# A token and channel mixer behind threshold attention: four small rearrangements in place of an interleaved second token layer

## The chip, the cores and the metric

The kernel runs on one core of a Trainium2 chip. A core has five engines that run beside each other and meet at semaphores: TensorE (PE, matmuls and transposes into PSUM), VectorE (DVE), ScalarE (ACT), GpSimd (POOL) and SyncE (SP, which here only issues DMAs). The metric is the device time of one launch in microseconds (us).

## The reference

Eight batch rows, eight heads, 576 tokens, 64 channels a head. Attention keeps only scores within `tau` of their row's maximum, and its output, put together to `[8, 576, 512]`, goes through a mixer with a token MLP (576 to 256 to 576) and a channel MLP (512 to 1536 to 512), each with a residual:

```python
scores = scale * q @ k.T
thresh = max(scores, -1) - tau
scores = where(scores >= thresh, scores, -1e9)
attn = softmax(scores);  x = attn @ v            # heads side by side: (8, 576, 512)
h = relu(x.T @ w_tok1) @ w_tok2                  # over tokens
u = x + h.T
out = u + relu(u @ w_ch1) @ w_ch2                # over channels
```

q, k, v are float32. The four weights are float64 and reach the kernel as 64-bit words, so they are converted to float32 on the chip.

## The kernel before

Work runs through *units*: 128 rows of scores for two heads, 18 units to a batch row, 144 in all (`u`; `t = u % 9`). In unit `u` the loop makes the scores of `u`, normalizes `u - 1`, and turns the weights of `u - 2` (`w`), so that they can be multiplied by the values when three units are together. Batch row 0 turns on PE (`turn`), the others on DVE in 32x32 blocks with DMAs behind them (`turn_blocks`). From row 1 on the mixer's steps of the row before are handed out between these by `fill`, each with a cost against a quota.

Loading queries and keys, and what runs at the start:

```python
nc.scalar.dma_start(out=tau_sb, in_=...)             # first on ACT's queue
def load_qk(n, eng, parts=range(8)):                 # part: 32 channels of one head, of q or k
    ...
        eng[which].dma_start(out=loaded[n][which][32*i : 32*i+32], in_=(q, k)[which][b, 2*p+h, :, 32*c : 32*c+32]...)
load_qk(0, (nc.sync, nc.scalar))                     # q on SP, k on ACT
... # five small DVE operations on tau_sb -> toff, ntau
def prep(n):                                         # q, then k, whole: 128x576 each
    for src, name in ((lq, "qT"), (lk, "kT")):
        nc.vector.transpose(out=sb, in_=src...)
prep(0)
```

Converting the weights: 31 pieces, each in three parts; `weight(n)` does the next n parts. Part 0 and 1 of piece i+1 stand on ACT beside the parts of piece i on DVE:

```python
def on_scalar(i, part):
    if part == 0: nc.scalar.activation(out=lo, in_=lo, func=AF.Copy, scale=2.0**-29)        # L193
    else:         nc.scalar.activation(out=h2, in_=hi, func=AF.Abs)                         # L195
def on_vector(i, part):
    if part == 0:   nc.vector.tensor_scalar(out=h2, in0=h2, ... max, mult)                  # L203
    elif part == 1: nc.vector.tensor_scalar(out=bits, in0=h2, ... shift)                    # L205
    else:           nc.vector.scalar_tensor_tensor(out=bits, in0=hi, ..., in1=bits)         # L209
def on_gpsimd(i):   nc.gpsimd.tensor_tensor(out=dst, in0=dst, in1=lo, op=ALU.add)           # L217
```

`h2` is one buffer (`high`) for all pieces. One pass of the loop, cut:

```python
scores(u)                    # PE matmuls L304; DVE maxima L309; POOL bias L310
...; norm(u - 1)             # DVE rr L333, L334; POOL L337
if b_now: weight(2)
...
if back and not in_blocks(wb):
    for i in range(3): turn(w, i)      # PE tr L355, copy to eT on DVE or ACT, L357
if b_now: fill(0.4)
if back and in_blocks(wb): turn_blocks(w)    # DVE L367, 16 DMAs L376
if b_now: weight(2)
weigh(u)                     # ACT Prelu L319, Exp L326, with fill(0.2) between
if b_now: weight(2)
```

The mixer: `turn_x` (PE tx L447, ACT copy L448) and `tok1` (PE L454), then `tok2`, whose add into xT is on DVE; `channel_mlp` has `ch1` (PE L510, ACT Relu L511) and `ch2` (PE L532, DVE add L544 or copy L550, store L551). PSUM for these comes from pools of two buffers.

```python
def tok2(c, f):              # 288 tokens (half f) of 128 channels (c): two matmul pairs, L464
    ...; nc.vector.tensor_add(out=u, in0=u, in1=to)                                         # L468
steps += [(0.97, lambda: tok2(c, f)) for f in range(2) for c in ps]
...
last = steps[-half:]; del steps[-half:]      # push(b): the second halves (f = 1) ...
for i, step in enumerate(steps):             # left-over steps of the row before go between
    n = (3 if b == 1 or (b % 2 == 0 and i == waits[1]) else 2) if i in waits else 1
    todo.extend(old[:n] + [step]); del old[:n]
...
for i, step in enumerate(last): new.insert(2*i + 1, step)    # ... stand between ch1 steps
```

`ch2` runs in parts of J = 3 products, but J = 1 in the second group of row pair 0.

Of the kernel before, what the change touches and what calls it, by code (L numbers as in the profile page):

```python
# [21 lines left out]
def kernel(  # L22
# [63 lines left out]
    UB = 9 * NP // 2  # L86

    tau_sb = const.tile([P, 1], F32, name="tau_sb")
    nc.scalar.dma_start(out=tau_sb, in_=bass.AP(tensor=tau.tensor, offset=0, ap=[[0, P], [1, 1]]))


    loaded = {}
    VL = 4
    vlast = [const.tile([P, P], F32, name=f"vl{i}") for i in range(VL)]

    def load_qk(n, eng, parts=range(8)):


        b, p = pairs[n]
        if n not in loaded:  # L100
            loaded[n] = [ld.tile([P, S // 32, 32], F32, tag=tag, bufs=1, name=f"{tag}_{n}") for tag in ("lq", "lk")]
        for part in parts:
            i, which = divmod(part, 2)
            h, c = divmod(i, 2)
            eng[which].dma_start(
                out=loaded[n][which][32 * i : 32 * i + 32],
                in_=(q, k)[which][b, 2 * p + h, :, 32 * c : 32 * c + 32].rearrange("(n t) d -> t n d", t=32),
            )

    def load_v(n):  # L110
# [8 lines left out]
    make_identity(nc, ident)  # L119
    for t in vlast:  # L120
        nc.gpsimd.memset(t, 0.0)
    load_qk(0, (nc.sync, nc.scalar))

    w1 = const.tile([P, NT, DTOK], F32, name="w1")
    w2 = const.tile([P, NTK, S], F32, name="w2")
# [10 lines left out]
    WMAX = 512  # L136
    scratch = work.tile([P, NP * 2 * S], U32, tag="xT", name="scratch")
    NRAW = 4
    high = scratch[:, 2 * WMAX * NRAW : 2 * WMAX * NRAW + WMAX].bitcast(F32)
    raw_at = [scratch[:, 2 * WMAX * i : 2 * WMAX * (i + 1)] for i in range(NRAW)]  # L140

    def like(x, dst):
# [26 lines left out]
    def load_piece(i):  # L169
        if i >= len(pieces):  # L170
            return
        dst, src = pieces[i]
        rows = dst.shape[0]
        n = 1
        for d in dst.shape[1:]:
            n *= d
        raw = raw_at[i % NRAW][0:rows, 0 : n * (2 if wide(i) else 1)].bitcast(src.dtype)
        nc.sync.dma_start(out=like(raw, dst), in_=src)
        if wide(i):
            words = raw.bitcast(U32).rearrange("p (n w) -> p n w", w=2)  # L180
            h2 = high[0:rows, 0:n]
            raws[i] = like(words[:, :, 0], dst), like(words[:, :, 1], dst), like(h2, dst)
        else:
            raws[i] = like(raw, dst)
# [77 lines left out]
    tlow = const.tile([P, 1], F32, name="tlow")  # L262
    toff = const.tile([P, 1], F32, name="toff")
    ntau = const.tile([P, 1], F32, name="ntau")
    nc.vector.tensor_scalar(out=tlow, in0=tau_sb, scalar1=0.0, scalar2=-3.0e38, op0=ALU.is_lt, op1=ALU.mult)
    nc.vector.tensor_scalar(out=toff, in0=tau_sb, scalar1=0.0, scalar2=FAR, op0=ALU.max, op1=ALU.min)
    nc.vector.tensor_scalar(out=toff, in0=toff, scalar1=-1.0 / SCALE, scalar2=None, op0=ALU.mult)
    nc.vector.tensor_add(out=toff, in0=toff, in1=tlow)
    nc.vector.tensor_scalar(out=ntau, in0=toff, scalar1=SCALE, scalar2=None, op0=ALU.mult)


    heads = {}
# [5 lines left out]
    def in_blocks(b):  # L278
        return b > 0

    def prep(n):
        lq, lk = loaded.pop(n)
        made = []
        for src, name in ((lq, "qT"), (lk, "kT")):
            sb = work.tile([P, S], F32, tag=name, name=f"{name}_{n}")
            nc.vector.transpose(out=sb, in_=src.rearrange("p n d -> p (n d)"))  # L286
            made.append(sb)
        heads[n] = made

    def scores(u):  # L290
        b, p0, t = units[u]
# [136 lines left out]
    def token_mlp(b, ps=range(NP)):  # L428

        xT = xTs[b]  # L430
        o = S * (b % 2)
        L = len(ps)
        cols = slice(P * ps[0], P * ps[0] + P * L)
        if b not in hidden:
            hidden[b] = work.tile([P, NTK, DM], F32, tag="a", bufs=1, name=f"a_{b}")
        a = hidden[b]

        def psum(name):
            return (ps_mm or ps_tr).tile([P, DM], F32, tag="mm" if ps_mm else "tr", name=name)

        def turn_x(t, n):
            M = MT[t]
            to = ps_tr.tile([P, MAIN], F32, tag="tr", name=f"tx_{b}_{t}_{ps[0]}")[0:M, 0 : n * L * P].rearrange("p (t c x) -> p t c x", t=n, c=L)
            for i in range(n):
                for c in range(L):
                    tok = o + (t + i) * P
                    nc.tensor.transpose(out=to[:, i, c, :], in_=xT[:, ps[c], tok : tok + M], identity=ident)  # L447
            nc.scalar.copy(out=x_sb[0:M, t : t + n, cols], in_=to.rearrange("q t p d -> q t (p d)"))  # L448

        def tok1(m):  # L450
            need(2)
            to = psum(f"t1_{b}_{m}_{ps[0]}")[:, 0 : P * L]
            for t in range(NT):
                nc.tensor.matmul(to, lhsT=w1[:, t, P * m : P * m + P], rhs=x_sb[:, t, cols], start=(t == 0), stop=(t == NT - 1))  # L454
            if ps_mm:
                nc.scalar.activation(out=a[:, m, cols], in_=to, func=AF.Relu)
            else:
                copies.append(lambda: nc.vector.tensor_scalar(out=a[:, m, cols], in0=to, scalar1=0.0, scalar2=None, op0=ALU.max))

        def tok2(c, f):  # L460
            need(6)
            to = psum(f"t2_{b}_{c}_{f}")[:, 0:HS]
            for m in range(NTK):
                nc.tensor.matmul(  # L464
                    to, lhsT=a[:, m, P * c : P * c + P], rhs=w2[:, m, HS * f : HS * f + HS], start=(m == 0), stop=(m == NTK - 1)
                )
            u = xT[:, c, o + HS * f : o + HS * f + HS]
            nc.vector.tensor_add(out=u, in0=u, in1=to)  # L468

        n = NI // L  # L470
        steps = [(0.11 * n * L, lambda t=t: turn_x(t, n)) for t in range(0, NI, n)] + [(0.11 * L, lambda: turn_x(NI, 1))]
        first = len(steps)
        steps += [(1.1 * L, lambda m=m: tok1(m)) for m in range(NTK)]
        steps += [(0.97, lambda c=c, f=f: tok2(c, f)) for f in range(2) for c in ps]
        return steps, (first, first + NTK)


# [4 lines left out]
    def channel_mlp(b, uT, i):  # L482
# [1 line left out]
        s = {}  # L484
        n = min(GR, 2 * S - GR * i)
        nt = n // P


        J = 1 if b == 0 and i == 1 else 3

        def turn_u():

# [22 lines left out]
                    s["ut"] = work.tile([P, GR // P, 4, NCC * 32], F32, tag="ut", bufs=1, name=f"ut_{b}_{i}")  # L515
                    turn_u()

        def ch2(t, part, J):

            need(7 + NJ + J * part + J - 1)  # L520
            t0 = GR * i + P * t
            if part == 0:
                s["ps"] = ps_mm.tile([P, NCC, P], F32, tag="mm", name=f"c2_{b}_{i}_{t}")
# [7 lines left out]
            for j in range(J * part, J * part + J):  # L531
                nc.tensor.matmul(  # L532
                    flat,
                    lhsT=s["g"][:, j, P * t : P * t + P],
                    rhs=wc2[:, j, :],
                    start=(j == 0 and b > 0),
                    stop=(j == NJ - 1),
                    skip_group_check=True,
                )
            if J * part + J == NJ:  # L540
                o = s["us"][:, t].rearrange("q a x -> q (a x)")
                if b:
                    move_u()
                    nc.vector.tensor_add(  # L544
                        out=o.rearrange("q (c k d) -> q c k d", c=NCC, k=4),
                        in0=ps.rearrange("q c (k d) -> q c k d", k=4),
                        in1=s["ut"][:, t].rearrange("q k (c d) -> q c k d", c=NCC),
                    )
                else:
                    nc.vector.tensor_copy(out=o, in_=flat)  # L550
                nc.sync.dma_start(out=out[b : b + 2].rearrange("b s d -> (b s) d")[t0 : t0 + P, :], in_=o)  # L551

        return [(0.0067 * n, lambda j=j: ch1(j)) for j in range(NJ)] + [
            (0.867 * J + (0.0 if part or b else 0.4), lambda t=t, part=part: ch2(t, part, J)) for t in range(nt) for part in range(NJ // J)
        ]

    def move_u():
# [25 lines left out]
    def push(b):  # L583
        nonlocal quota
        uT = xTs[b]
        steps, waits = token_mlp(b) if b else token_mlp(b, range(NP // 2, NP))
        half = NP if b else NP // 2
        last = steps[-half:]
        del steps[-half:]
        old = list(todo)  # L590
        todo.clear()
        todo.extend(early)
        early.clear()

        for i, step in enumerate(steps):
            n = (3 if b == 1 or (b % 2 == 0 and i == waits[1]) else 2) if i in waits else 1
            todo.extend(old[:n] + [step])
            del old[:n]
        todo.extend(old)
        new = []  # L600
        for i in range(2) if b % 2 == 0 else range(2, (2 * S + GR - 1) // GR):
            new.extend(channel_mlp(b - b % 2, uT, i))

        for i, step in enumerate(last):
            new.insert(2 * i + 1, step)
        todo.extend(new)
        quota = (sum(c for c, _ in todo) - (KEEP if b else KEEP_FIRST)) / (UB - 1)

    prep(0)
    due = deque()  # L610
    b_now = 0
    LAG = 2
# [13 lines left out]
    for u in range(len(units) + LAG + 4):  # L626
# [18 lines left out]
            early.popleft()[1]()  # L645
        if 0 < u <= len(units):
            norm(u - 1)
        if b_now:
            weight(2)
        else:  # L650


# [21 lines left out]
        if back and in_blocks(wb):  # L674
            turn_blocks(w)
        if b_now:
            weight(2)
        if on and (b_now or not visit):
            weigh(u)
        elif b_now:  # L680
# [60 lines left out]
```

## Time and profile before

| | before |
|---|---|
| time, median of 3 | 1360.13 us (1359.4 to 1361.83) |
| span of the profiled execution | 1360.0 us |
| PE busy | 1310.5 us (96%) |
| DVE, ACT, POOL busy | 590.9, 584.4, 354.8 us |
| half-clock stretches of PE[...] | near 100, 114, 141 and 250 us |

PE's busy time against the span says how much room is left, and the stretches show where it is. A row of the waits names who waited for whom, the total, the number of times and the longest. In the timeline a row has its start, its length, the engine with the line of the kernel, what it writes and reads, and in brackets the idle time of that engine ahead of it with what ended it. SPq and ACTq are DMA issues.

### The profile page before, as it was taken

What the parts mean: (1) busy time and instruction counts of PE and PEld (TensorE: products, weight loads), DVE (VectorE), ACT (ScalarE), POOL (GpSimd) and SP (SyncE); (2) the same over time, 40 slices, a digit from 0 to 9 for tenths busy, and PEclk for the clock granted to TensorE, in tenths of its full rate; (3) what the DMA queues carried; (4) which work ended last, traced back from release to release, by engine and by line L of the source; (5) the groups of instructions that cost most, each with busy time, mean ns of one, the idle gap of its engine ahead of it and who ended that gap; (6) DMA issues with size and microseconds to landing.
All of it is one profiled execution on the core that took longest, in us unless ns stands there. A gap on an engine that the chain in (4) does not pass through costs nothing.

```text
span 1360.0 us, 17797 instructions
## 1 busy us (share of the span) xinstructions
PE 1310.5 (96%) x6138; PEld 812.2 (60%) x6138; DVE 590.9 (43%) x1024; ACT 584.4 (43%) x1299; POOL 354.8 (26%) x683
## 2 busy tenths in 40 slices
PE   6888899999999999999999999999999999999998
PEld 4555656547474666565665567465757566576675
DVE  5878874445343553435244445434443454201000
ACT  5776654454454444443434534353434454220110
POOL 4665652222222221222122222222221222100000
PEclk9998999999999999999999999999999999999999
DMA  5434764545454444444344435534443452400000
GB/s 122 109 90 125 203 157 103 127 95 124 93 126 99 104 112 100 112 110 100 82 104 110 116 83 124 124 81 113 110 101 83 113 117 76 112 24 22 18 24 32
DMA packets 296538, 135.31 MB, mean 99 GB/s; under 512 B 204736, under 2 KB 289216, under 8 KB 296448
## 3 DMA queue, kind: packets, MB, share of 16 engines
q1 hardware_dynamic: 167840, 118.15, 34.1%
q10 hardware_dynamic: 128608, 16.01, 7.4%
q8 instruction: 49, 0.80, 0.3%
q14 instruction: 41, 0.34, 0.1%
HBM read 43.25 MB, written 9.44 MB: 39 GB/s over the span
## 4 chain that ended last, share of the span: by engine, by line
PE 82%; DVE 5%; DMA 4%; ACT 3%; SPq 3%; issue 1%; POOL 1%; ACTq 0%; DVEq 0%; POOLq 0%
PE c L532 26%; PE c L510 24%; PE sc L304 10%; PE pv L416 8%; PE t L454 5%; PE t L464 4%; PE pv L411 3%; DVE mx L309 2%; SPq L376 2%; DMA lq<-in_q_dram 2%; ACT e L319 1%; SPq L500 1%; PE tx L447 1%; DMA lk<-in_k_dram 1%; ACT e L326 1%
## 5 line engine op out<-in xcount | busy, mean ns | idle before, releaser
L309 DVE TENSOR_REDUCE mx<-sc 128x1 f32<-128x576 f32 x288 | 204.4, 750 | 488.6 <-PE sc L304 488.5
L510 PE MATMUL c<-xT,wc 128*128 128x256 f32 (+1 forms) x1920 | 402.3, 362 | 6.2 <-DVE xT L468 3.3
L532 PE MATMUL c<-wc,g 128*128 128x512 f32 x864 | 388.8, 597 | 0.0
L510 PEld LDWEIGHTS c<-xT,wc 128*128 128x128 f32 x1920 | 333.7, 190 | 73.9 <-issue 24.2
L310 POOL TENSOR_SCALAR bias<-mx,toff 128x1 f32<-128x1 f32 x288 | 83.2, 289 | 781.8 <-DVE mx L309 725.5
L532 PEld LDWEIGHTS c<-wc,g 128*128 128x128 f32 x864 | 158.6, 190 | 184.2 <-issue 182.2
L319 ACT ACTIVATE e<-sc,bias 128x576 f32<-128x576 f32 x288 | 199.3, 740 | 151.4 <-POOL bias L310 147.1
L511 ACT ACTIVATE g<-c 128x256 f32<-128x256 f32 (+1 forms) x240 | 87.0, 363 | 314.7 <-PE c L510 307.8
L326 ACT ACTIVATE e<-e,ntau 128x576 f32<-128x576 f32 x288 | 221.3, 772 | 0.0
L337 POOL TENSOR_SCALAR e<-e,rr 128x576 f32<-128x576 f32 x288 | 215.1, 760 | 14.1 <-DVE rr L334 3.3
L304 PE MATMUL sc<-kT,qT 64*128 64x288 f32 (+1 forms) x1280 | 194.2, 440 | 12.2 <-DVE kT L286 7.3
L367 DVE STREAM_TRANSPOSE T<-e 128x1152 f32<-128x1152 f32 x126 | 171.9, 1364 | 5.2 <-DMA eT<-T 2.1
L304 PEld LDWEIGHTS sc<-kT,qT 64*128 64x128 f32 (+1 forms) x1280 | 107.1, 180 | 98.0 <-issue 54.6
L416 PE MATMUL pv<-eT,lv 128*64 128x384 f32 (+1 forms) x1024 | 138.6, 411 | 0.0
L416 PEld LDWEIGHTS pv<-eT,lv 128*64 128x64 f32 x1024 | 77.8, 139 | 49.5 <-issue 42.9
L421 ACT COPY xT<-pv 128x384 f32<-128x384 f32 (+1 forms) x56 | 21.0, 401 | 180.2 <-PE pv L416 172.9
L544 DVE TENSOR_TENSOR us<-c,ut 128x512 f32<-128x512 f32 x27 | 18.7, 692 | 156.0 <-PE c L532 135.4
L464 PE MATMUL t<-w,a 128*128 128x288 f32 x256 | 76.3, 422 | 1.4 <-DVE xT L468 1.3
L454 PE MATMUL t<-x_sb,w 128*128 128x512 f32 (+1 forms) x180 | 73.8, 558 | 0.0
L464 PEld LDWEIGHTS t<-w,a 128*128 128x128 f32 x256 | 46.4, 192 | 22.2 <-issue 10.6
L326 ACT ACTIVATION_READ_ACCUMULATOR e<-e,ntau 128x1 f32 x288 | 56.9, 198 | 0.0
L411 PE MATMUL pv<-eT,vl 128*64 128x384 f32 (+1 forms) x256 | 46.6, 433 | 10.5 <-DMA lq<-in_q_dram 3.6
(46 smaller groups left out, 525.6 us busy)
## 6 DMA issues: line engine op xcount, KB each, us to landing
eT<-T SPq DMA_DIRECT2D x672, 108.0 KB, 2.3
scratch<-in_moe_w_ch_dram SPq DMA_DIRECT2D x24, 512.0 KB, 3.7
lv<-in_v_dram SPq DMA_DIRECT2D x32, 288.0 KB, 3.3
out_dram<-us SPq DMA_DIRECT2D x36, 256.0 KB, 2.2
lk<-in_k_dram ACTq DMA_DIRECT2D x111, 72.0 KB, 2.8
lq<-in_q_dram ACTq DMA_DIRECT2D x106, 72.0 KB, 2.3
ut<-us SPq DMA_DIRECT2D x192, 32.0 KB, 1.9
lq<-in_q_dram SPq DMA_DIRECT2D x22, 72.0 KB, 3.3
```

The lines of the kernel that those rows point to most:

```text
L304: nc.tensor.matmul(sc[h][rows, f, 0:HS], lhsT=qT[r, cols], rhs=kT[r, HS * f : HS * f + HS], start=True, stop=True)
L309: nc.vector.tensor_reduce(out=mx[:, c], in_=sc[h][:, :, 0:HS], axis=AX.XY, op=ALU.max)
L319: nc.scalar.activation(out=eh, in_=sc[h][:, :, 0:HS], func=AF.Prelu, bias=bias[:, h : h + 1], scale=SCALE, alpha=STEEP)
L326: nc.scalar.activation(out=eh, in_=eh, func=AF.Exp, bias=ntau, accum_out=rs[:, h : h + 1])
L337: nc.gpsimd.tensor_scalar(out=eh, in0=eh, scalar1=rr[:, h : h + 1], scalar2=1.0, op0=ALU.mult, op1=ALU.mult)
L367: nc.vector.transpose(out=T[:, :, place, :].rearrange("p a (c x) -> p c a x", c=NK), in_=e.rearrange("p (c a x) -> p c a x", c=NK, a=4))
L411: nc.tensor.matmul(to[r], lhsT=vl[:, r], rhs=e[NI], start=True, stop=False, skip_group_check=True)
L416: nc.tensor.matmul(to[r], lhsT=lv[:, j, :], rhs=e[j], start=False, stop=(c == NI - 1), skip_group_check=True)
L454: nc.tensor.matmul(to, lhsT=w1[:, t, P * m : P * m + P], rhs=x_sb[:, t, cols], start=(t == 0), stop=(t == NT - 1))
L464: nc.tensor.matmul(to, lhsT=a[:, m, P * c : P * c + P], rhs=w2[:, m, HS * f : HS * f + HS], start=(m == 0), stop=(m == NTK - 1))
L510: nc.tensor.matmul(ps, lhsT=wc1[:, j, c, :], rhs=uT[:, c, GR * i : GR * i + n], start=(c == 0), stop=(c == NCC - 1))
L532: nc.tensor.matmul(flat, lhsT=s["g"][:, j, P * t : P * t + P], rhs=wc2[:, j, :], start=(j == 0 and b > 0), stop=(j == NJ - 1), skip_group_ ...
```

## The change

There are five parts. The last takes something out again that the kernel before had.

- **First unit's queries.** The first 128 queries are loaded by DMAs of their own and transposed alone ahead of the keys; the other 448 follow, on the same queue. `tau` is loaded behind the keys, and its five DVE operations come behind the transposes.
- **Two places for absolute values.** `high` becomes a buffer of twice the size; piece i uses half `i % 2`. It lies in space that the channel MLP takes later.
- **Row 0's last turns.** In units 18 and 19, in which row 0's last two units are turned, the first `weight(2)` moves behind the turns, as `weight(4)` with the one that stood there.
- **Last tile in column halves.** The second channel layer of the last 128 tokens runs as twelve products of 256 columns, add and store, and then the same for the other 256.
- **The token MLP's second layer** is not split any more: its steps run channel group by channel group, both halves in turn, all ahead of the channel MLP. The special cases of n and J go.

```diff
-    load_qk(0, (nc.sync, nc.scalar))
+    load_qk(0, (nc.sync, nc.scalar), blocks=(range(P // 32), range(S // 32)))
+    load_qk(0, (nc.sync, None), range(0, 8, 2), blocks=(range(P // 32, S // 32), None))
+    nc.scalar.dma_start(out=tau_sb, ...)
...
-    high = scratch[:, 2 * WMAX * NRAW : 2 * WMAX * NRAW + WMAX].bitcast(F32)
+    high = work.tile([P, GR // P, 4, NCC * 32], F32, tag="ut", bufs=1, name="high")...
...
-            h2 = high[0:rows, 0:n]
+            h2 = high[0:rows, WMAX * (i % 2) : WMAX * (i % 2) + n]
...
+        for which, lo, hi in ((0, 0, first), (1, 0, S // 32), (0, first, S // 32)):   # prep(0, 4)
+            if lo < hi: nc.vector.transpose(out=heads[n][which][:, 32*lo : 32*hi], in_=srcs[which][:, lo:hi]...)
...
-        steps += [(0.97, lambda c=c, f=f: tok2(c, f)) for f in range(2) for c in ps]
+        steps += [(0.97, lambda c=c, f=f: tok2(c, f)) for c in ps for f in range(2)]
...
-        J = 1 if b == 0 and i == 1 else 3
...
+        def ch2_last(half):
+            ps = ps_mm.tile([P, w], F32, tag="mm", ...)                    # w = 256
+            for j in range(NJ): nc.tensor.matmul(ps, lhsT=s["g"][:, j, 0:P], rhs=wc2[:, j, w*half : w*half + w], ...)
+            if half == 0: move_u()
+            nc.vector.tensor_add(out=o..., in0=ps..., in1=s["ut"]...)
+            nc.sync.dma_start(out=out[...][t0 : t0 + P, w*half : w*half + w], in_=o)
...
-            n = (3 if b == 1 or (b % 2 == 0 and i == waits[1]) else 2) if i in waits else 1
+            n = 2 if i in waits else 1
...
-        for i, step in enumerate(last): new.insert(2 * i + 1, step)
...
+        turns_left = b_now and back and not in_blocks(units[w][0])
         if b_now:
-            weight(2)
+            if not turns_left: weight(2)
...
         if b_now:
-            weight(2)
+            weight(4 if turns_left else 2)
```

More of the change, by code (lines that the diff above doesn't have):

```diff
@@ L88 @@
     tau_sb = const.tile([P, 1], F32, name="tau_sb")
-    nc.scalar.dma_start(out=tau_sb, in_=bass.AP(tensor=tau.tensor, offset=0, ap=[[0, P], [1, 1]]))
     loaded = {}
@@ L94, with load_qk @@
     vlast = [const.tile([P, P], F32, name=f"vl{i}") for i in range(VL)]
-    def load_qk(n, eng, parts=range(8)):
+    def load_qk(n, eng, parts=range(8), blocks=(range(S // 32),) * 2):
         b, p = pairs[n]
@@ L104, in load_qk @@
             h, c = divmod(i, 2)
+            lo, hi = blocks[which].start, blocks[which].stop
             eng[which].dma_start(
-                out=loaded[n][which][32 * i : 32 * i + 32],
-                in_=(q, k)[which][b, 2 * p + h, :, 32 * c : 32 * c + 32].rearrange("(n t) d -> t n d", t=32),
+                out=loaded[n][which][32 * i : 32 * i + 32, lo:hi],
+                in_=(q, k)[which][b, 2 * p + h, 32 * lo : 32 * hi, 32 * c : 32 * c + 32].rearrange("(n t) d -> t n d", t=32),
             )
@@ L121 @@
         nc.gpsimd.memset(t, 0.0)
-    load_qk(0, (nc.sync, nc.scalar))
+    load_qk(0, (nc.sync, nc.scalar), blocks=(range(P // 32), range(S // 32)))
+    load_qk(0, (nc.sync, None), range(0, 8, 2), blocks=(range(P // 32, S // 32), None))
+    nc.scalar.dma_start(out=tau_sb, in_=bass.AP(tensor=tau.tensor, offset=0, ap=[[0, P], [1, 1]]))
     w1 = const.tile([P, NT, DTOK], F32, name="w1")
@@ L138 @@
     NRAW = 4
-    high = scratch[:, 2 * WMAX * NRAW : 2 * WMAX * NRAW + WMAX].bitcast(F32)
+    high = work.tile([P, GR // P, 4, NCC * 32], F32, tag="ut", bufs=1, name="high").rearrange("q n a x -> q (n a x)")
     raw_at = [scratch[:, 2 * WMAX * i : 2 * WMAX * (i + 1)] for i in range(NRAW)]
@@ L264 @@
     ntau = const.tile([P, 1], F32, name="ntau")
[L265 to L269, printed above, removed]
     heads = {}
@@ L279, in in_blocks, with prep @@
         return b > 0
[L281 to L288, printed above, removed]
+    def prep(n, first=S // 32):
+        srcs = loaded.pop(n)
+        heads[n] = [work.tile([P, S], F32, tag=name, name=f"{name}_{n}") for name in ("qT", "kT")]
+        for which, lo, hi in ((0, 0, first), (1, 0, S // 32), (0, first, S // 32)):
+            if lo < hi:
+                nc.vector.transpose(
+                    out=heads[n][which][:, 32 * lo : 32 * hi], in_=srcs[which][:, lo:hi].rearrange("p n d -> p (n d)")
+                )
     def scores(u):
@@ L516, in ch1, with ch2 @@
                     turn_u()
-        def ch2(t, part, J):
-            need(7 + NJ + J * part + J - 1)
+        def ch2(t, part):
+            need(7 + NJ + 3 * part + 2)
             t0 = GR * i + P * t
@@ L530, in ch2 @@
                     )
-            for j in range(J * part, J * part + J):
+            for j in range(3 * part, 3 * part + 3):
                 nc.tensor.matmul(
@@ L539, in ch2 @@
                 )
-            if J * part + J == NJ:
+            if part == 3:
                 o = s["us"][:, t].rearrange("q a x -> q (a x)")
@@ L551, in ch2 @@
                 nc.sync.dma_start(out=out[b : b + 2].rearrange("b s d -> (b s) d")[t0 : t0 + P, :], in_=o)
+        def ch2_last(half):
+            t0 = GR * i
+            w = DM // 2
+            ps = ps_mm.tile([P, w], F32, tag="mm", name=f"c2_{b}_{i}_h{half}")
+            for j in range(NJ):
+                nc.tensor.matmul(
+                    ps, lhsT=s["g"][:, j, 0:P], rhs=wc2[:, j, w * half : w * half + w], start=(j == 0), stop=(j == NJ - 1)
+                )
+            if half == 0:
+                move_u()
+            o = s["us"][:, half].rearrange("q a x -> q (a x)")[:, 0:w]
+            cs = slice(NCC // 2 * half, NCC // 2 * half + NCC // 2)
+            nc.vector.tensor_add(
+                out=o.rearrange("q (c k d) -> q c k d", c=NCC // 2, k=4),
+                in0=ps.rearrange("q (c k d) -> q c k d", c=NCC // 2, k=4),
+                in1=s["ut"][:, 0].rearrange("q k (c d) -> q c k d", c=NCC)[:, cs],
+            )
+            nc.sync.dma_start(out=out[b : b + 2].rearrange("b s d -> (b s) d")[t0 : t0 + P, w * half : w * half + w], in_=o)
+        if b == B - 2 and n == P:
+            return [(0.0067 * n, lambda j=j: ch1(j)) for j in range(NJ)] + [(5.2, lambda half=half: ch2_last(half)) for half in range(2)]
         return [(0.0067 * n, lambda j=j: ch1(j)) for j in range(NJ)] + [
-            (0.867 * J + (0.0 if part or b else 0.4), lambda t=t, part=part: ch2(t, part, J)) for t in range(nt) for part in range(NJ // J)
+            (2.6 if part or b else 3.0, lambda t=t, part=part: ch2(t, part)) for t in range(nt) for part in range(4)
         ]
@@ L586, in push @@
         steps, waits = token_mlp(b) if b else token_mlp(b, range(NP // 2, NP))
-        half = NP if b else NP // 2
-        last = steps[-half:]
-        del steps[-half:]
         old = list(todo)
@@ L599, in push @@
         todo.extend(old)
-        new = []
         for i in range(2) if b % 2 == 0 else range(2, (2 * S + GR - 1) // GR):
[L602 to L606, printed above, removed]
+            todo.extend(channel_mlp(b - b % 2, uT, i))
         quota = (sum(c for c, _ in todo) - (KEEP if b else KEEP_FIRST)) / (UB - 1)
-    prep(0)
+    prep(0, P // 32)
+    nc.vector.tensor_scalar(out=tlow, in0=tau_sb, scalar1=0.0, scalar2=-3.0e38, op0=ALU.is_lt, op1=ALU.mult)
+    nc.vector.tensor_scalar(out=toff, in0=tau_sb, scalar1=0.0, scalar2=FAR, op0=ALU.max, op1=ALU.min)
+    nc.vector.tensor_scalar(out=toff, in0=toff, scalar1=-1.0 / SCALE, scalar2=None, op0=ALU.mult)
+    nc.vector.tensor_add(out=toff, in0=toff, in1=tlow)
+    nc.vector.tensor_scalar(out=ntau, in0=toff, scalar1=SCALE, scalar2=None, op0=ALU.mult)
     due = deque()
@@ L647 @@
             norm(u - 1)
+        turns_left = b_now and back and not in_blocks(units[w][0])
         if b_now:
-            weight(2)
+            if not turns_left:
+                weight(2)
         else:
```

## The prediction

> **What bounds the kernel now.** I read the engine table first, then busy time by stage, then the waits and the timeline of the stages in which TensorE (PE) is not full. The engine table:
>
> ```profile
> PE 1310.5 (96%) x6138; PEld 812.2 (60%) x6138; DVE 590.9 (43%) x1024; ACT 584.4 (43%) x1299; POOL 354.8 (26%) x683
> ```
>
> PE is busy 1310.5 of 1360.0 us. The change neither adds nor removes PE work (the last tile's matmuls are only cut narrower), so at most 49.5 us can move. By stage (columns: stretch, length, then busy time and count of PE, weight loads, DVE, ACT, POOL, then granted clock, DMA share, GB/s):
>
> ```profile
> 0.00:20.00 20.00, 11.05 (x31) 6.83 (x32) 7.86 (x19) 8.72 (x17) 6.15 (x22) 1.00 0.76 162
> 20.00:34.00 14.00, 12.43 (x64) 7.46 (x66) 11.86 (x26) 11.22 (x25) 8.46 (x15) 1.00 0.31 64
> 34.00:68.00 34.00, 28.91 (x199) 18.26 (x195) 28.13 (x62) 26.81 (x59) 20.96 (x34) 1.00 0.47 109
> 68.00:102.00 34.00, 27.99 (x184) 17.90 (x185) 27.06 (x57) 26.54 (x55) 21.11 (x32) 0.98 0.37 90
> 102.00:136.00 34.00, 29.02 (x128) 18.44 (x131) 27.59 (x51) 21.61 (x43) 18.56 (x23) 0.87 0.45 125
> 136.00:170.00 34.00, 29.39 (x141) 20.44 (x134) 29.57 (x48) 22.40 (x48) 20.57 (x27) 0.95 0.76 203
> ...
> 510.00:714.00 204.00, 201.65 (x928) 124.08 (x927) 82.61 (x138) 84.14 (x189) 46.14 (x98) 1.00 0.43 101
> ```
>
> The last row stands for the rest: from 170 us on PE is nearly full. Length minus PE in the first six rows is 9.0 + 1.6 + 5.1 + 6.0 + 5.0 + 4.6 = 31.3 us, so 31 of the 49.5 idle us lie before 170 us, where weights are converted beside the attention of batch row 0. In 34 to 170 us DVE is busy 112.4 of 136 us (83%): no engine is full[...]. After 170 us the idle time is some 14 us in short gaps, and 3.8 us in the tail. So each part of the change is worth single microseconds.
>
> [...] at 97.51 us ACT's L195 ends a wait of 1.97 us for DVE, and the Prelu behind it starts only at 98.09 although its bias was ready at 96.2.[...] The trace has granted clocks of 0.66 in 100 to 105 us and 0.50 in 115 to 120 us, behind sparse stretches.[...] DVE's L205 takes from 404 to 1403 ns for one shape, long when POOL's L217 runs.
>
> **The change, part by part.**
>
> 1. *Start.* Before:
>
> ```profile
> 0.73 0.42 ACTq L89 DMA_DIRECT2D tau_sb<-in_tau_dram  x1
> 1.17 2.77 ACTq L105 DMA_DIRECT2D lk<-in_k_dram  x4
> 6.45 0.78 DVE L286 STREAM_TRANSPOSE kT<-lk 128x576 f32<-128x576 f32 x1
> ```
>
> The chain goes through the keys: lk's last DMA lands just ahead of 6.45, and the first matmul starts at 7.28, at kT's end. With tau behind them the keys are issued 0.44 us earlier, and share the DMA engines with 4 instead of 18 query blocks at first. The rest of the queries (some 0.6 us of transpose, from 0.78 us for 576) and the five tau operations (0.7 us) fall in the 2.3 us before the first reduction at 9.60, so they are hidden. Gain 0.4 to 1.0: **-0.6**.
>
> 2. *Two places for the absolute values.* Piece i+1's Abs (ACT L195) no longer waits until DVE's L205 has read piece i's. The waits removed, from the list for 34 to 172 us:
>
> ```profile
> ACT scratch L195 <- DVE wc L205: 7.2, 6, 2.0
> ACT scratch L195 <- DVE w L205: 3.4, 2, 2.5
> ```
>
> That is 10.6 us of ACT waiting. But ACT is 64 to 79% busy there, and what PE then waits for is mostly DVE. At 97.51 us, for instance, the next PE transposes (99.22) waited for DVE's copy, behind L209, and not for ACT. DVE's work stays the same. I count a fifth of 10.6: **-2**.
>
> 3. *Row 0's last turns first.* In the loop's units 18 and 19 the copies to eT go ahead of two conversion steps. At unit 19:
>
> ```profile
> 113.64 0.54 DVE L357 COPY eT<-tr 128x384 f32<-128x384 f32 x1
> 114.23 0.75 PE L355 MATMUL tr<-ident,e 128*128 128x128 f32 x3 [2.64 <-DVE eT L357]
> ```
>
> DVE did L203 and L205 (112.41 to 113.71) before the copy that PE wanted; without them the copy starts 1.2 us earlier: -1.2. At unit 18 it costs: those two steps used to fill 103.4 to 104.3 us while PE was still at L454; now they come after the copies: +0.85, of which the third transpose gains some 0.3 back: +0.5. The half-clock stretch behind unit 19 (some 6.8 us; chain PE work of 2.92 + 1.48 + 3.51 + 2.15 us in it) would be worth about 3 us if the denser PE work avoided it; I give that 0.3: -0.9. Sum **-1.5**.
>
> 4. *The token MLP's second layer, in a row again.* The order of instructions shows little: from row 3 on eight of these steps still alternate with left-over channel steps. In row 2 they do not. At unit 41 four groups of turns (tx) follow each other; two PSUM buffers take them, and ACT copies the third's predecessor only behind two Prelus (1.4 us). Laid out from before's durations, PE waits from some 3.1 to 4.5 us after unit 41's scores start: +1.5. At unit 44 five of the second layer's steps come together. Before had
>
> ```profile
> 305.70 1.24 PE L464 MATMUL t<-w,a 128*128 128x288 f32 x4 [1.26 <-DVE xT L468]
> ```
>
> with DVE's 1.37 us transpose in front of the two adds; that stays, and the same happens once more at unit 44, where I find 0.8. Gaps of 0.2 and 0.55 us at 310 and 318 us go with the interleaving: -0.75. Later rows: the step J = 3 instead of 1 and the new positions move whole 2.6 us steps between units, and with them the short waits of the values' matmuls for eT (2.35 us near 538, 0.6 near 755, and so on): work moves into the first and out of others (units 93 and 138), I put -0.6 with an error of 3. Sum 1.5 + 0.8 - 0.75 - 0.6, about **+1**.
>
> 5. *Tail.*
>
> ```profile
> 1345.77 10.46 PE L532 MATMUL c<-wc,g 128*128 128x512 f32 x24
> 1356.27 0.69 DVE L544 TENSOR_TENSOR us<-c,ut 128x512 f32<-128x512 f32 x1 [17.46 <-PE c L532]
> 1356.99 0.34 SPq L551 DMA_DIRECT2D out_dram<-us  x1
> ```
>
> Per column 128-wide matmuls took 11.04 / 96 / 128 = 0.90 ns and 512-wide ones 10.46 / 24 / 512 = 0.85 ns, so the same columns in 48 halves should take 10.5 to 10.9 us. The first half's add and store lie beside the second half. The last add is half as wide (some 0.35 us less) and the last store half as large (some 0.3 less; a 256 KB store lands in 2.2 us, a 16 KB copy in 1.8, so most of that is fixed). Less 0.1 on PE: **-0.5**.
>
> Sum: -0.6 - 2 - 1.5 + 1 - 0.5 = -3.6, so 1360.1 - 3.6 = **1356.5 us**.
>
> **The rivals.** (a) *Hidden*: DVE carries 83% of the conversion stage and its work is the same, so ACT's removed waits come back as waits for DVE. For it: the 97.51 us case. Against: ACT also carries Prelu and Exp, which release score buffers, and PE waits for them in that stage (3.6 us). It would give about 1359. (b) *The removed interleaving bites*: waits as at 305.70 come at every row's second layer. For it: DVE's 1.37 us transposes and 1.42 us reductions stand between the adds in every unit. Against: channel steps stand between most. It would give 1362 to 1366. (c) *The conversion stage unlocks*: PE stays dense enough to avoid the half-clock stretches at 100 and 114 us, and ACT's 10.6 us come through by half. It would give 1350.
>
> **Range and chances.** The terms' own errors are about 0.5, 2, 2, 3 and 0.3, together some 4.3 us; 8 in 10 would be 5.5 to either side, and I widen it for whole clock windows: 1350 to 1364. Two per cent are 27 us, more than half of all PE idle time, so within 2% has 0.97, faster 0.02, slower 0.01.
>
> **What would show it.** Start: first matmul at 6.3 to 6.9 us. Abs: no wait of ACT for L205's successor, while DVE's waits and busy share in 34 to 170 us tell (a) from (c). Turns: PE's wait at unit 19 at most 1.5 us; the clock in 110 to 125 us. Second layer: a gap of 1 to 2 us in PE near 285 us, and waits of its steps for DVE xT of 2 us in all instead of 1.3. Tail: last DVE add about 0.35 us, from its end to the span's end some 2.7 us instead of 3.1. PE busy stays at 1310 us. It is wrong if the gaps after 170 us grow or shrink by over 5 us in all, or if half-clock windows are added or lost.

## The result and the profile after

The changed kernel takes 1355.67 us against 1359.78 us of the kernel before (medians of six runs each): ratio 0.9969, 95% interval 0.9956 to 0.9982, that is 4.2 us less, between 2.4 and 6.0. A second series on another chip gave 0.9959 (0.9943 to 0.9974). The prediction was 1356.5 us, 3.6 us less. The total was right, but its terms were not; the experiments show by how much each was off.

The engine table of the page after: PE's work is what it was, and the span is shorter around it.

```profile
span 1354.5 us, 17840 instructions
...
PE 1310.0 (97%) x6162; PEld 816.0 (60%) x6162; DVE 593.4 (44%) x1026; ACT 584.9 (43%) x1299; POOL 353.3 (26%) x683
```

Busy time by stage after (columns as in the prediction):

```profile
34.00:68.00 34.00, 28.65 (x188) 18.14 (x186) 26.61 (x60) 25.85 (x57) 20.80 (x34) 0.95 0.45 106
68.00:102.00 34.00, 28.51 (x188) 19.76 (x184) 27.73 (x58) 26.83 (x55) 20.69 (x32) 0.95 0.37 90
102.00:136.00 34.00, 29.76 (x141) 18.61 (x143) 29.26 (x52) 21.73 (x44) 18.46 (x24) 0.90 0.46 126
136.00:170.00 34.00, 30.59 (x142) 21.33 (x134) 29.71 (x47) 22.11 (x48) 20.58 (x26) 0.90 0.76 203
...
510.00:714.00 204.00, 204.00 (x939) 125.15 (x937) 86.69 (x143) 87.32 (x195) 47.91 (x102) 1.00 0.44 102
```

Two things stand in it that the prediction did not have. From 34 to 170 us PE is busy 117.5 us against 115.3 before, but its clock is lower (0.95, 0.95, 0.90, 0.90 against 1.00, 0.98, 0.87, 0.95): it does about the same work at a lower speed, and unit 26 comes no earlier than before (+0.5 us). From 510 to 714 us PE is never idle; before it was idle for 2.35 us there. In these traces the gain lies behind 200 us, where I had put a loss.

To follow the shift from place to place I use one small instruction that each unit has, the DVE reciprocal of `norm(u)`, and subtract its start in before from that in the other kernel. For the changed kernel: -0.1 us at unit 0, +1.5 at 11, +1.9 at 19, 0.0 at 20, +0.5 at 26, -0.1 at 71, -2.5 at 78, -4.0 at 117, -5.2 at 143. In the tail another 0.6 goes, but spans of single executions differ by 1 to 2 us, so each step had to be tested.

### The profile page after: what moved, and what is told of

Its sections match the earlier page's. It is cut to its first block, busy times and chain, and to the rows that moved or that the text cites. A ratio compares the mean times of both kernels' runs of the same rounds, so it can differ in the third digit from the quotient of the medians.

```text
span 1354.5 us, 17840 instructions
## 1 busy us (share of the span) xinstructions
PE 1310.0 (97%) x6162; PEld 816.0 (60%) x6162; DVE 593.4 (44%) x1026; ACT 584.9 (43%) x1299; POOL 353.3 (26%) x683
## 4 chain that ended last, share of the span: by engine, by line
PE 86%; DVE 5%; ACT 4%; DMA 2%; SPq 1%; issue 1%; POOL 0%; ACTq 0%; DVEq 0%; POOLq 0%
PE c L528 26%; PE c L507 26%; PE sc L304 11%; PE pv L416 8%; PE t L454 5%; PE t L464 4%; PE pv L411 3%; DVE mx L309 2%; ACT e L319 1%; PE tr L355 1%; PE tx L447 1%; ACT e L326 1%; DMA lk<-in_k_dram 1%; PE c_h L555 1%; SPq L376 1%
## 5 line engine op out<-in xcount | busy, mean ns | idle before, releaser
L528 PE MATMUL c<-wc,g 128*128 128x512 f32 x840 | 379.0, 597 | 0.0
L528 PEld LDWEIGHTS c<-wc,g 128*128 128x128 f32 x840 | 154.4, 190 | 176.3 <-issue 172.6
L337 POOL TENSOR_SCALAR e<-e,rr 128x576 f32<-128x576 f32 x288 | 213.9, 755 | 14.3 <-ACT g L508 2.6
L468 DVE TENSOR_TENSOR xT<-xT,t 128x288 f32<-128x288 f32 x64 | 28.3, 446 | 71.1 <-PE t L464 70.6
```

Source lines behind the costliest of these rows:

```text
L337: nc.gpsimd.tensor_scalar(out=eh, in0=eh, scalar1=rr[:, h : h + 1], scalar2=1.0, op0=ALU.mult, op1=ALU.mult)
L528: nc.tensor.matmul(flat, lhsT=s["g"][:, j, P * t : P * t + P], rhs=wc2[:, j, :], start=(j == 0 and b > 0), stop=(j == NJ - 1), skip_group_ ...
```

## The experiments

Theory A, from this trace: the second layer's place makes the gain, and the conversion's two parts and PE's clock only cancel. Rival B, from the prediction: the start, the two places, the turns and the tail make it, and the second layer costs. Most parts were taken alone first; the start and the tail first ran together.

**The second layer alone.**

```diff
-steps += [... for f in range(2) for c in ps]          # and: second halves between the ch1 steps, n = 3, J = 1
+steps += [... for c in ps for f in range(2)]          # all ahead of the channel MLP, n = 2, J = 3
```

> Only the fifth part, the token MLP's second layer in a row again (with n and J as after). First theory: this part makes most of the gain, by work moved between units behind 200 us; then the time is 3 to 4.5 us below before, unit 20's DVE reciprocal stands within 1 us of before's, and the shift builds up in steps after unit 36 to some -4 us at unit 131. Rival: the gain is the sum of the other four parts, as most of the prediction's sum had it; then this alone is +1 us against before, within 1.

Measured: 1357.81 us, ratio 0.9976 (0.9968 to 0.9984), that is -3.3 us. Theory A holds. Unit 20 stands at +0.6, and the shift goes to -3.8 at unit 78 and -4.8 at 143. What PE waits for behind 170 us, in before:

```profile
PE pv L411 <- DMA lq<-in_q_dram: 3.6, 2, 2.7
PE c L510 <- ACT g L511: 2.7, 4, 0.8
PE pv L411 <- DMA lv<-in_v_dram: 2.4, 1, 2.4
PE pv L411 <- DMA eT<-T: 1.8, 2, 1.4
...
PE pv L411 <- DMA out_dram<-us: 0.6, 1, 0.6
```

and with the second layer alone:

```profile
PE t L464 <- ACT g L511: 3.2, 3, 1.6
PE pv L411 <- DMA lq<-in_q_dram: 1.9, 1, 1.9
PE t L464 <- DVE xT L468: 1.8, 2, 1.3
PE tx L447 <- ACT x_sb L448: 1.5, 2, 1.2
PE sc L304 <- ACT e L319: 0.9, 1, 0.9
...
PE pv L411 <- DMA out_dram<-us: 0.4, 1, 0.4
PE pv L411 <- DMA eT<-T: 0.4, 1, 0.4
```

The values' products (pv) waited 8.4 us for transfers and now wait 2.7: -5.7. The row names only the transfer that ended last; pv does not read queries, so a row with lq tells when, and not what. Against that stand new waits: 1.5 for the copies to x_sb behind the turns, 0.9 of scores for the Prelu, and 0.5 more on Relu and the second layer's adds together. With 0.4 less under `issue`, the net of these two traces is -3.2.

That this is so near to the measured -3.3 is in part chance, because the waits differ from trace to trace. In the seven traces with the old order (before twice, and the runs below that leave it) pv waits 6.4 to 8.4 us for transfers (mean 7.7), in the five with the new (this one, the changed kernel twice and two variants of it below) 2.7 to 6.1 (mean 4.5), and all of PE's listed waits behind 170 us are 13.3 against 11.4 us in the mean. So waits show some 2 of the 3.3 us; the rest is not assigned. The effect itself is in every trace: from unit 36's reciprocal to unit 143's it takes 904.6 to 906.8 us in the seven (mean 905.5) and 901.3 to 903.3 us in the five (mean 902.0), that is 3.4 us less, and the start, the two places and the turns are found in both groups.

How the largest wait went, in the timelines near 538 us. Before:

```profile
523.40 11.96 SPq L376 DMA_DIRECT2D eT<-T  x16
524.07 5.45 PE L510 MATMUL c<-xT,wc 128*128 128x256 f32 x24
...
538.39 0.55 PE L411 MATMUL pv<-eT,vl 128*64 128x192 f32 x4 [2.35 <-DMA lv<-in_v_dram]
```

After:

```profile
522.18 11.04 SPq L376 DMA_DIRECT2D eT<-T  x16
522.26 7.17 PE L507 MATMUL c<-xT,wc 128*128 128x256 f32 x32
...
535.88 0.55 PE L411 MATMUL pv<-eT,vl 128*64 128x192 f32 x4
```

From the first eT transfer's issue to the products are 15.0 us before, 2.35 of them idle, and 13.7 after with none: four of the channel MLP's groups of matmuls now stand in that stretch instead of three, and SP is done with its sixteen issues sooner. In all, PE works 12.6 us in the stretch before and 13.7 after, and the last of the sixteen transfers lands 14.6 us behind the first issue before and 12.8 after. The quicker landing is of this group alone: over all 42 groups of a trace the landing takes 13.0 to 13.1 us in the mean, with the old order and with the new. The transfers are not faster on the whole; more of PE's work lies where it would have waited for them. This gap is in all seven traces with the old order (1.2 to 2.35 us) and in none of the four with the new order and J = 3.

**Two places alone.**

```diff
-h2 = high[0:rows, 0:n]
+h2 = high[0:rows, WMAX * (i % 2) : WMAX * (i % 2) + n]
```

> Only the two places for absolute values. The prediction's step: -2 us, seen as an earlier unit 19. First theory now: nothing (within 0.5 us), because DVE carries the conversion stage and ACT's wait only turns into another. Rival: it costs 1.5 us by unit 11, as the changed kernel's trace has it, whatever PE's clock does. Third: the 1.5 us in the changed kernel were a half-clock stretch of PE at 59 us that comes and goes; then unit 19's shift here goes with the half-clock stretches ahead of it and not with the waits.

Measured: 1360.15 us against 1361.16, ratio 0.9993 (0.9984 to 1.0001): -1.0 us, and nothing is not excluded. ACT's waits from 34 to 172 us:

```profile
ACT scratch L193 <- DMA scratch<-in_moe_w_ch_dram: 11.8, 5, 6.3
ACT eT L357 <- PE tr L355: 8.7, 8, 2.0
ACT a L456 <- PE t L454: 7.7, 3, 5.0
```

The 10.6 us for L205 are gone. But ACT waits 11.8 us for raw weights instead of 6.3, 8.7 for PE's turns instead of 5.6, and 7.7 instead of 6.6 for the first token layer: 9.7 of the 10.6 us came back behind other names. All of ACT's listed waits together are 37.7 us instead of 38.9. The rival's 1.5 us by unit 11 did not come: this trace is 1.7 us late at unit 0 already, and 1.9 at unit 11.

**The turns alone, and with the two places.**

```diff
-weight(2);  ... turn(w, i) ...;  weight(2)            # units 18 and 19
+            ... turn(w, i) ...;  weight(4)
```

> Only row 0's last turns ahead of the conversion. First theory: -1 to -2 us between units 18 and 21 (PE's wait for DVE's copy at unit 19, 2.64 us before, falls under 1.5), and about as much at the end. Rival: units 18 to 21 only shift work on DVE, which has no idle time to give; then unit 22 stands within 0.5 us of before's.

Measured: 1368.0 us, ratio 1.0047 (1.0031 to 1.0063): +6.4 us. Neither theory had that. In the trace 2.8 us of it stand between unit 17 and unit 20. At unit 19 of this kernel:

```profile
118.05 0.56 DVE L357 COPY eT<-tr 128x384 f32<-128x384 f32 x1 [0.64 <-PE tr L355]
118.98 1.39 DVE L205 TENSOR_SCALAR wc<-scratch 128x512 uint32<-128x512 uint32 x1
...
120.40 0.67 ACT L195 ACTIVATE scratch<-scratch 128x512 f32<-128x512 f32 x1 [2.46 <-DVE wc L205]
120.97 1.35 ACT L319 ACTIVATE e<-sc,bias 128x576 f32<-128x576 f32 x2
...
121.75 2.91 PE L304 MATMUL sc<-kT,qT 64*128 64x288 f32 x8 [3.73 <-ACT e L319]
```

L205 now comes behind the copies; with one place ACT's Abs (L195) must wait for it (2.46 us), the Prelu behind it in ACT's order starts only at 120.97, and PE's next scores wait 3.73 us for the Prelu to free their PSUM. In the changed kernel the same place reads:

```profile
114.43 0.55 PE L355 MATMUL tr<-ident,e 128*128 128x128 f32 x3 [0.64 <-DVE eT L357]
...
115.34 1.36 ACT L319 ACTIVATE e<-sc,bias 128x576 f32<-128x576 f32 x2
115.94 1.39 DVE L209 TENSOR_SCALAR wc<-high 128x512 uint32<-128x512 uint32 x1
116.12 2.28 PE L304 MATMUL sc<-kT,qT 64*128 64x288 f32 x8 [1.14 <-ACT e L319]
```

The Prelu starts before that DVE step (line L209 there), and PE waits 1.14 us. If that edge is the cost, the two parts belong together, which the next run tests.

> Only the two places and the turns, together. Alone they measured -1.0 and +6.4 us. First theory: they add up, and this is +5 us. Rival: the turns cost only through the one place (ACT's Abs waits 1.39 and 2.46 us for an L205 that now comes late, and PE's scores wait 2.98 and 3.73 us behind it); then PE's wait for the Prelu at units 18 and 19 stays near 1.3 us each, and this is -2 to 0 us.

Measured: 1360.13 us against 1359.53, ratio 0.9999 (0.9989 to 1.0009): -0.1 us. They do not add up (+5 was expected then), and PE's two waits for the Prelu are 1.45 and 1.15 us, as the rival had them: the cost of the turns was the one place. But a gain of the turns does not show either: the two places alone had -1.0. The traces show where it went. PE's wait for DVE's copy at unit 19 did fall, from 2.64 us in before to 0.64 in the changed kernel. But its waits for the Prelu there and at unit 18 rose from none and 1.07 us to 1.14 and 1.45, because ACT now has two conversion steps instead of one between its copy and the Prelu. That takes some 1.5 of the 2.0 us back.

> The changed kernel without its third part (row 0's last turns stay behind the first conversion step). First theory: the turns cost even with two places for the absolute values; then this is about 3 us faster than the changed kernel, 6 to 8 us below before. Rival: with two places the turns cost nothing, because ACT's Abs no longer stands behind DVE's L205, and they gain the 1 to 2 us of the prediction; then this is 0 to 2 us slower than the changed kernel, 2.5 to 4 us below before.

The diff of this one is the change without the lines of `turns_left`. Measured: 1353.05 us, ratio 0.9953 (0.9940 to 0.9966), -6.4 us. It is the fastest kernel by its ratio, 0.8 and 2.2 us below the changed kernel's two series, but the intervals overlap: that the turns still cost something with two places is suggested and not settled. The rival, under which this kernel is the slower one and 2.5 to 4 us below before, does not fit. Over the stretch in which they act, from unit 17's reciprocal to unit 20's, against before: -3.9, -1.7, -1.7 us in the three kernels with two places and the old order, +0.1, -1.6, -2.1 in the three with both. A gain of the turns would have to stand there.

**The two ends.**

```diff
+load_qk(0, ..., blocks=(range(4), range(18)));  ...;  tau behind        # start
+ch2_last(half)                                                          # tail
```

> The first unit's queries and tau behind the keys, and the last tile in column halves; the two lie at the two ends of the trace and are read there. First theory, from the changed kernel's trace: the first reduction 0.1 us earlier, the time from the last tile's first product to the span's end 0.6 us shorter; 0.5 to 0.8 us in all. The prediction's step: 0.6 and 0.5, that is 1.1 us in all.

Measured: 1359.02 us, ratio 0.9980 (0.9972 to 0.9988): -2.7 us, more than either.

> Only the first unit's queries and tau behind the keys. Together with the last tile's halves it measured -2.7 us, of which the trace showed 0.6 at the end and 0.1 to 0.2 at the first reduction. First theory: the start moves the later loads and the clock windows, and brings another 1 to 2 us between units 3 and 28. Rival: it brings only what the first reduction shows, 0 to -0.3 us, and the rest was chance of the half-clock windows.

Measured: 1358.08 us, ratio 0.9987 (0.9979 to 0.9995): -1.8 us. The rival falls, and the theory is right in size, but the place is the start itself. It is worth more than the one pair of traces showed, because the kernel before has a wide start, and its first trace was a lucky one. The keys' transpose begins at 6.35, 6.45, 7.35, 7.80, 7.81 and 8.18 us in six traces with the old loading, and at 5.86, 5.88, 6.12, 6.23, 6.24 and 6.33 in six with the new. Unit 0's reciprocal comes 1.2 us earlier in the mean (six traces each). Two traces, the old start in the turns' kernel and the new one in the changed kernel:

```profile
7.81 0.78 DVE L286 STREAM_TRANSPOSE kT<-lk 128x576 f32<-128x576 f32 x1 [1.45 <-DMA lk<-in_k_dram]
```

```profile
0.72 3.21 ACTq L105 DMA_DIRECT2D lk<-in_k_dram  x4
...
6.33 0.78 DVE L286 STREAM_TRANSPOSE kT<-lk 128x576 f32<-128x576 f32 x1 [1.80 <-DMA lk<-in_k_dram]
```

The tail, after:

```profile
1340.84 10.53 PE L555 MATMUL c_h<-wc,g 128*128 128x256 f32 x48
1346.22 0.42 DVE L562 TENSOR_TENSOR us<-c_h,ut 128x256 f32<-128x256 f32 x1 [12.51 <-PE c_h L555]
...
1351.40 0.42 DVE L562 TENSOR_TENSOR us<-c_h,ut 128x256 f32<-128x256 f32 x1 [4.75 <-PE c_h L555]
```

From the last tile's first product to the span's end are 13.7 us instead of 14.3: -0.6. The two runs' difference, -2.7 less -1.8, agrees within their intervals.

**Nothing changed.**

> The kernel before, unchanged, for a second trace. If the half-clock stretches of PE stand where the program is sparse, they come at 100, 114, 141 and 250 us again, within a microsecond, and unit 28 within 0.5 us; if their place in time is free of the program, they come elsewhere, and unit 28 moves by 1 to 3 us with nothing changed.

Measured: 1360.96 us. The half-clock stretches move, though unit 28 moves by only 0.3 us. In the first trace of before:

```profile
247.60:251.00 3.40, 0.91 (x3) 0.08 (x1) 0.00 (x0) 1.95 (x5) 0.20 (x1) 0.99 0.88 188
251.00:254.40 3.40, 3.21 (x21) 2.75 (x22) 0.00 (x0) 0.00 (x0) 0.00 (x0) 0.50 0.45 92
...
534.30:537.70 3.40, 1.74 (x5) 0.43 (x3) 0.00 (x0) 0.49 (x2) 0.00 (x0) 1.00 1.03 229
```

and in the second:

```profile
246.80:250.20 3.40, 1.73 (x5) 0.43 (x3) 0.66 (x1) 2.77 (x6) 1.02 (x2) 1.00 0.73 159
250.20:253.60 3.40, 2.32 (x29) 2.35 (x31) 0.00 (x0) 0.00 (x0) 0.00 (x0) 1.00 0.70 138
...
533.50:536.90 3.40, 1.45 (x11) 0.65 (x11) 0.00 (x0) 0.00 (x0) 0.00 (x0) 1.00 0.90 195
536.90:540.30 3.40, 3.40 (x25) 3.22 (x23) 0.00 (x0) 0.00 (x0) 0.00 (x0) 0.50 0.00 0
```

The third but last column is the clock. The stretch at 251 us is gone, and with it 1.5 us between units 35 and 36; one at 537 us is new.

The times at which the clock changes show more. From 30 us to just before the end they are, in the first trace, 100.8, 104.2, 114.4, 121.3, 141.7, 145.2, 251.0 and 254.4 us, in the second 106.8, 120.5, 141.0, 144.4, 164.9, 168.3, 536.9 and 540.3 us: in each trace all are whole steps of 3.41 us apart, but the steps of the two do not coincide (their first changes are 6.0 us, or 1.76 steps, apart). In the first trace PE's gap at 250 us falls into one step (busy 0.91 of 3.40 us), and half clock follows. In the second it is split between two steps (1.73 and 2.32 us), and none follows. In the first traces of before and of the changed kernel together, PE went from full to half clock nine times from 30 us to just before the end, each time behind a step in which it was busy for 23 to 59%. It stayed at full clock behind 15 other steps in which PE was busy for 52 to 69%, and behind all 738 with more. In two of the nine stretches half clock went on for a second step, with PE busy for 96 and 80% of the first. So the gap at 250 us is in both traces of before, but its place among the steps is not the same.

> The changed kernel again, for its time beside the others on one chip and for a second trace. Its first interval was 1.8 to 4.4 thousandths below before... that is 2.4 to 6.0 us; expected 4 us. If the half-clock stretches at 58 and 75 us belong to the change they come again; if not, unit 12 stands 1.5 us earlier than in the first trace.

Measured: 1354.42 us, ratio 0.9959 (0.9943 to 0.9974). The stretch at 58 us did not come again; the one at 75 us did, from 74.0 to 77.4. First trace of the changed kernel, then the second:

```profile
57.40:60.80 3.40, 2.21 (x10) 1.80 (x11) 3.37 (x9) 3.03 (x7) 1.92 (x5) 0.80 0.67 176
60.80:64.20 3.40, 3.40 (x16) 1.36 (x15) 2.79 (x7) 3.40 (x9) 2.74 (x5) 0.70 0.56 116
```

```profile
57.40:60.80 3.40, 3.40 (x21) 1.93 (x22) 3.37 (x9) 3.31 (x8) 2.96 (x5) 1.00 0.82 200
60.80:64.20 3.40, 3.22 (x23) 1.52 (x19) 1.97 (x7) 3.40 (x8) 2.98 (x4) 1.00 0.79 198
```

Unit 12 stands at -1.7 instead of +1.5 us. Of these 3.2 us, 0.4 are there at unit 0, another 1.1 come between units 1 and 3, and 1.6 between units 6 and 11, where the stretch was. So the first trace's loss there does not come with every execution. Whether the change makes it more frequent stays open: of the four traces of the changed kernel and its variants without the turns, three have the stretch near 58 us and all have the one near 75; of the six with some of the parts, two have stretches between 40 and 82 us, and the two of before have none.

**Two attempts to go on.**

```diff
-    nc.sync.dma_start(out=eT[...], in_=T[...])                        # all 16 of a group of three units
+    i < 2: nc.sync.dma_start(...)  else, after weigh(u): nc.scalar.dma_start(...)
```

> The kernel before, with the sixteen transfers from T to eT issued by two queues: eight by SP as before, eight by ACT after the unit's Prelu and Exp. First theory: the second layer's place gains because PE waits less for these transfers (8.4 us after 170 us before, 2.7 with the second layer alone), and they are late because one queue needs 11 to 13 us to issue them; then PE's waits for transfers behind 170 us fall under 3 us, and the time by 3 to 6 us, with the second layer where it was. Rival: the landing is what counts, or ACT's issues (some 0.4 us each) delay Prelu and Exp by as much; then the waits move to scores on Prelu and the time stays within 2 us.

Measured: 1508.11 us, ratio 1.1077 (1.1057 to 1.1096), 147 us slower. ACT's waits:

```profile
ACT g L518 <- DMA eT<-T: 104.3, 16, 9.4
ACT e L319 <- DMA eT<-T: 103.8, 15, 9.6
```

PE's list behind 170 us has no wait of pv for a transfer any more, but 74.1 us for Relu and 19.2 for Prelu. An issue of these on ACT takes some 0.65 us (1.25 us for two and 2.82 us for four in the timeline), most of the eight come in a row, and what stands behind them on ACT waits. In this kernel the issues are paid in ACT's order; whether SP's issue time or the landing is what makes eT late stays open, because the cost hides it.

> The changed kernel without the turns, with eT's transfers on two queues. If the second layer's place and the two queues take away the same wait, this is within 1.5 us of the changed kernel without the turns (6.4 us below before); if they add, it is 8 to 11 us below before.

Measured: 1496.86 us, ratio 1.0998 (1.0977 to 1.1020), for the same reason; it tells nothing on whether the two gains are one.

> The changed kernel without the turns and with J = 1 again for the second group of row pair 0, so that unit 41's turns have products between them. The prediction's step: PE's wait for ACT's x_sb copies (1.5 us, seen at 285 to 287 us) goes, and the time with it, to 7.5 to 8.5 us below before. Rival: the work between the turns only moves the wait to the values' products of unit 39 and after; then it is within 0.5 us of the version with J = 3.

```diff
-J = 3
+J = 1 if b == 0 and i == 1 else 3                    # on top of the version without the turns
```

Measured: 1355.11 us, ratio 0.9954 (0.9940 to 0.9968), -6.3 us: the same as with J = 3. PE's 1.5 us for x_sb went from the list, and its waits for transfers are 5.6 us instead of 4.2. The total says little (2.7 to 6.1 in the four traces with J = 3), but one wait can be named: pv waits 1.69 us for eT at 388.8 us. All seven traces with the old order, and so with J = 1, have a gap there (1.0 to 1.6 us), and none with J = 3 has. The rival holds: one wait in the place of the other.

## Why the prediction was right or wrong, point by point

| part | predicted | measured |
|---|---|---|
| start | -0.6 | -1.8 (-2.9 to -0.7) |
| two places | -2 | -1.0 (-2.2 to +0.1) |
| turns, given two places | -1.5 | +0.8 (-1.0 to +2.6), pair less two places; alone +6.4 |
| second layer | +1 | -3.3 (-4.4 to -2.2) |
| tail | -0.5 | -0.6 in the trace |
| all | -3.6 | -4.2 (-6.0 to -2.4), again -5.6 (-7.8 to -3.5) |

The measured terms, with the pair as one, add to -5.8, inside both intervals of the whole. That the total of the prediction came out right is luck: the two conversion parts gave 3.4 us less than forecast, the second layer 4.3 and the start 1.2 us more.

- *Bound.* Right: PE busy stayed at 1310 us, and every effect was single microseconds. That most of the gain would come from the first 170 us, where most of the idle time lay, was wrong: idle time tells where there is room, not where this change acts.
- *Start.* The mechanism was right, and the size was off. I read one trace of before, in which the keys landed early. Its term is the keys' landing, 1.2 us earlier in the mean instead of the 0.6 I took. The first product starts at 6.69 to 7.17 us in six traces (forecast 6.3 to 6.9) against 7.14 to 9.01 us in six with the old loading.
- *Two places.* The step "I count a fifth of 10.6" was right in kind (rival (a), hidden) and about twice too large: nine tenths came back as other waits.
- *Turns.* Wrong. The step that failed is the one that looked at DVE and PE alone ("without them the copy starts 1.2 us earlier"). The copy did start earlier, and PE's wait for it fell from 2.64 to 0.64 us. But the third engine's order was left out: the moved L205 releases ACT's Abs, and behind that stand Prelu and PE's scores (3.73 us of waiting in the run of the turns alone). With two places that edge is gone, and still the later Prelu takes some 1.5 of the 2.0 us back. The 0.3 given to an avoided half-clock stretch was an estimate, and could not be checked against chance.
- *Second layer.* Row 2 was right: PE's two waits for x_sb at unit 41 came (1.5 us in all), the one of 1.26 us for the adds stayed, and a second of 0.5 came instead of 0.8. What failed is the sentence on later rows, "I put -0.6 with an error of 3". The gap near 538 us went, as the sentence allows, but the losses that it set against it at units 93 and 138 did not come, and two gaps that it does not name, at 390 and 854 us (1.39 and 0.94 us in before), went too (no gap over 0.1 us there in the four traces with J = 3). With the other terms at some +1.3 in the waits, the later rows gave about -4.5 us, an estimate from the measured -3.3. There PE's work moved into stretches in which pv had waited for transfers, as near 538 us: 7.7 us of these waits in the mean with the old order, 4.5 with the new.
- *Tail.* Right: 0.42 us instead of 0.69 for the last add, 10.53 us for 48 products, 0.6 us in all.
- *Rivals.* (a) is what happened to the two places. (b) did not come: PE waits 1.8 us for the second layer's adds instead of 2.0, and that part alone is 3.3 us faster. (c) did not come: the clock after is 0.90 from 102 to 170 us, against 0.87 and 0.95 before, and the half-clock stretches move about with nothing changed.
- *Clock.* "Behind sparse stretches" is what the first traces of before and after show: PE was busy for 23 to 59% of the 3.41 us ahead of each of the nine stretches of half clock.

## What to carry to other kernels

When the bound engine has gaps, ask for each gap which transfer or engine it waits for, and how much of the bound engine's own work stands between that transfer's cause and its use; here such a move was worth 3.3 us. Before an operation is moved later on one engine, list all that it releases on the others: the same move cost 6.4 us with one buffer and nothing that could be measured with two, and its gain on one engine was taken back by another. And for effects of a microsecond, take several traces of the unchanged kernel first, since a single one decides which start, which waits and which clock you believe in.

## What the runs showed of the hardware that I had not expected

PE's clock fell to half behind a given gap in one execution of the same program and not in the next: with nothing changed, the stretches began near 101, 114, 142 and 251 us in one trace and near 107, 141, 165 and 537 us in the other. In each of the two traces the changes of the clock are whole steps of 3.41 us apart, with the steps of one trace off those of the other (1.76 steps between their first changes). With the stretch at 251 us went 1.5 us between two units, as much as most parts of this change. The first loads are as loose: with the same program text at the start, the transpose of keys that are issued from 1.17 us on began between 6.35 and 8.18 us. And with half of the eT transfers issued by ACT instead of SP, the kernel took 1508.11 us, 147 us more.
